# Loading q of batches 2 to 7 by four tokens of a head pair: 24 transfers of 128 KB for 48 of 64 KB, in a fused attention and feed-forward kernel

## The chip, the cores and the metric

The kernel runs on one core of a Trainium2 chip. The metric is the device time of one launch in microseconds (us). Three runs of the kernel before took 359.70, 361.41 and 361.73 us; the median is 361.41 us.

## What is computed

The inputs are q, k and v (8 batches, 8 heads, 576 tokens, head size 64, float32), a feature matrix `w_phi` (64 x 128) and the two matrices of a feed-forward network. Attention is linear: a feature map takes the place of the softmax.

```python
def phi(x):
    proj = np.einsum('bhsd,df->bhsf', x, w_phi)
    proj = proj - np.max(np.abs(proj), axis=-1, keepdims=True)
    return np.concatenate([np.exp(proj), np.exp(-proj)], axis=-1)
q_p, k_p = (phi(q), phi(k))
kv = np.einsum('bhsf,bhsd->bhfd', k_p, v)
z = np.sum(k_p, axis=2)
num = np.einsum('bhsf,bhfd->bhsd', q_p, kv)
den = np.einsum('bhsf,bhf->bhs', q_p, z)[..., None] + 1e-06
attn = num / den
...
x = np.ascontiguousarray(attn_out.transpose(0, 2, 1, 3)).reshape(B * S, H * D)
h = np.maximum(x @ w_in, 0.0)
return (h * h @ w_out).astype(np.float32)
```

`w_in` is 512 x 2048 and `w_out` 2048 x 512, so x has 4608 rows of 512 and the output has the same shape.

## The kernel before, in words

**Stages.** The 576 tokens of a batch are split into 512 and 64. Attention runs batch by batch (`attention(b)`). The feed-forward network runs over nine chunks of 512 rows: chunks 0 to 7 are the 512 tokens of each batch, chunk 8 collects the 64 left over of all eight. The main loop emits attention of batch c+1, the first matmul of chunk c (`ffn_in`, L692; `ffn_in_small`, L703, for chunk 0) and the second of chunk c-1 (`ffn_out`, L757) into one list, so attention of the next batch fills gaps of the feed-forward matmuls on TensorE (PE).

**Who does what.** GpSimd (POOL) issues all loads from memory, with a cast from float32 to bf16 (`load`, L245 and L253; `load_q`, L265). SyncE (SP) issues the transposes done by DMA (L317 for k and q of batches 2 to 7, L612 for the attention output `xo` into `xT` or `xS`) and the stores of the output (L775 for chunks 0 to 7, L772 for chunk 8). For batches 0 and 1, k and q are transposed on PE (L307). VectorE (DVE) and ScalarE (ACT) take the results out of PSUM: maxima (L388, L489), exponentials (L394, L539), relu (L669 or L671) and square (L678), scaling of v (L421), and the copy of the output into one of three buffers `ot` (`copy`: L192 on ACT, L190 on DVE). A copy into `ot` waits for the store of three copies earlier that read the same buffer.

**The end.** The last row tile of chunk 8 is computed in two halves (`last_out`, L721). The copies of the halves into `otl` (L735 on DVE, L737 on ACT) are followed by four small stores (L744): per half, one on SP's queue and one on ACT's. The other three row tiles of chunk 8 have two stores each (L772), all six on SP.

**Order.** Every operation is recorded with `add` and gets a number in the sequence of recording. `ORDER` is a list of these numbers written out by hand: the operations are issued in that order, and each engine works through its own in order. `STATES` says which of two engines takes an operation that may run on either, `BASES` gives each PSUM tile its bank. Loads of batches 2 to 7 are recorded with `release=True`, and nearly all are listed in `GATES`: such a load also waits for a given earlier operation. `FILL` gives, for 13 places ahead of operations of the first 21 us, a bank and a number of matmuls on a tile of zeros (`warm`, L825) that compute nothing.

**q.** `xq` (two buffers) holds q of a batch as 128 partitions by 36 x 64 elements. Partition p holds tokens 4p to 4p+3 of each head. In the kernel before, the two halves of a batch, jj = 0 and 1, are loaded apart: jj holds tokens 4p+2jj and 4p+2jj+1, so each head gives 128 elements in a row. For batches 2 to 7 a half comes in four pieces of one head pair (`PIECES`), which makes 8 transfers of 64 KB and two small ones (L253) for the 64 tokens left over. A block of 128 columns of `xq`, transposed, is one block t of `qT`; `q_ts(c)` lists the blocks of row tile c, the projections L333 read them one by one, and L524 reads four of them as one moving operand.

The SP queue carries, for each batch from 2 on, one transpose of the whole of `xk` and one of the whole of `xq`; the latter waits for all pieces of q.

Of the kernel before, what the change touches and what calls it, by code (L numbers as in the profile page):

```python
# [7 lines left out]
F32 = mybir.dt.float32  # L8
# [16 lines left out]
def dve_cost(n):  # L25
    return n / 960 + 0.064, n / 960 + 0.150 + SEM

# [80 lines left out]
def kernel(  # L108
# [52 lines left out]
    warm = sb("warm", [P])  # L161
# [9 lines left out]
    NXT = 2  # L171
    assert B * S == NCH * TCH and NCH == B + 1 and S == TCH + 64
    qp, qn = ring("qp", NQP, [8 * P]), ring("qn", NQP, [8 * P])
    xo = ring("xo", 3, [8 * D])
    rden = ring("rden", 3, [8], F32)
# [11 lines left out]
    def copy(out, in_):  # L187

        if now[0].eng == "DVE":
            pin(nc.vector.tensor_copy(out=out, in_=in_))  # L190
        else:
            pin(nc.scalar.activation(out=out, in_=in_, func=ACT.Copy))  # L192

# [65 lines left out]
    def load_q(b, jjs=(0, 1), single=True, release=False, prs=((0, 4),)):  # L259

        x = xq[b % 2]
        for jj in jjs:
# [10 lines left out]
    def of(tag, b, us):  # L273
        qs = [("xq", b % 2, u, a) for u in us if u != "s" for a in range(3)] if tag == "xq" else []
        return qs + [(tag, b % 2, u) for u in us if u != "s"] + [(tag, b % 2, "s", hi) for u in us if u == "s" for hi in range(2)]
# [19 lines left out]
    def attention(b):  # L295
# [122 lines left out]
        def scaled(t, x, n):  # L418

            e = t[:, :, D:].to_broadcast([t.shape[0], n, 2, D // 2]).rearrange("p m c x -> p m x c")  # L420
            pin(nc.vector.tensor_tensor(out=t[:, :, :D].rearrange("p m (x c) -> p m x c", c=2),  # L421
                                        in0=x.rearrange("p (m x c) -> p m x c", m=n, c=2), in1=e, op=ALU.mult))

        def v_ops(g0, g1):

            gs = [4] if g0 == 4 else list(range(g0, g1))
            for sg in range(2):
# [9 lines left out]
                def fn(t=t):  # L437
                    scaled(t[:, 8 * g0 : 8 * g1, :], xv[s2][:, 512 * g0 : 512 * g1], 8 * (g1 - g0))
                add("DVE", dve_cost(256 * (g1 - g0)), fn, r=of("xv", b, gs) + [("ve", s2, sg, g) for g in gs],
                    w=[("va", s2, sg, g) for g in gs], what="V")  # L440
# [28 lines left out]
        def q_ts(c):  # L469
            if c == 4:  # L470
                return [16, 17]
            return [8 * (c // 2) + h for h in range(8)] if first else [8 * (c // 2) + 4 * (c % 2) + i for i in range(4)]
# [36 lines left out]
        def q_ops(c):  # L509
# [3 lines left out]
            def fn():  # L513
                o = ps2(pf)
                for u in range(2):
# [5 lines left out]
                    else:  # L521
                        r = slice(64 * u, 64 * u + 64)
                        rhs = qTb[r, ts[0] : ts[-1] + 1, :]
# [19 lines left out]
        def out_ops(c):  # L543
# [27 lines left out]
            xs = xslot[0] % 3  # L571
# [92 lines left out]
    def relu_sq(g, dst, toks):  # L664
# [9 lines left out]
        def fn():  # L674
# [3 lines left out]
            pin(nc.vector.tensor_tensor(out=dst, in0=i_, in1=i_, op=ALU.mult))  # L678
        add("DVE", dve_cost(256), fn, r=[("hr", sl)], w=toks, what="sq")
# [6 lines left out]
    def ffn_in(c, mc):  # L686
# [8 lines left out]
        relu_sq(g, h2[c % 2][mc // 4][:, mc % 4, :], [("h2", c % 2, mc, tt) for tt in range(4)])  # L695

    def ffn_in_small(c, tt, mg):
# [10 lines left out]
        relu_sq(g, h2[c % 2][mg][:, :, tt * P : (tt + 1) * P], [("h2", c % 2, mg * 4 + i, tt) for i in range(4)])  # L708
# [39 lines left out]
    def ffn_out(c, tt, part):  # L748
# [12 lines left out]
        if part == 3:  # L761
# [6 lines left out]
            for u in range(2 if c == NCH - 1 else 1):  # L768
                def fn(u=u):
                    if c == NCH - 1:  # L770
                        b = 2 * tt + u
                        pin(nc.sync.dma_start(out=out[b * S + 512 : b * S + 576, :], in_=ot[sl][u * 64 : u * 64 + 64, :]))  # L772
# [3 lines left out]
                add("SP", (0.5, 0), fn, r=[("ot", sl)], dma=(0.37 if c == NCH - 1 else 0.74, HW_IN, "st"), what="st")  # L776
# [43 lines left out]
    for op in plan.arrange():  # L820
        if op.seq in FILL:
            now[0] = filler
            bank, n = FILL[op.seq]
            for _ in range(n):
                pin(nc.tensor.matmul(out=psum[:, bank, :P], lhsT=warm, rhs=warm, start=True, stop=True))  # L825
# [153 lines left out]
```

## Time and profile before

| | |
|---|---|
| three runs | 359.70, 361.41, 361.73 us |
| span of the profiled execution | 358.8 us (first to last instruction) |
| its own time beside the span | not given; the three runs are 0.9, 2.6 and 2.9 us above this span |
| PE busy | 341.0 us, 95% of the span |
| DVE, ACT, POOL busy | 276.7, 227.1, 112.8 us |
| granted TensorE clock | 0.997 on the mean |
| DMA packets | 102631, 39.62 MB |

How to read it: the span is cut into 40 slices on the profile's page; a digit is the busy share of a slice in tenths. A group of instructions is given by its line in the kernel, its engine, its operation and the tiles that it writes and reads, with the busy time, the mean duration and the idle time of the engine just ahead of it. "POOLq", "SPq" and "ACTq" stand for the sequencers that issue transfers; the time of a transfer itself is that from issue to landing. The chain of waits follows the work that ended last back through what released it.

### The profile page before, as it was taken

The numbers are of one execution on the slowest core, as the hardware profiler recorded it, in microseconds if no ns is written. First come the engines' busy times: TensorE is split into PE (matmuls) and PEld (weight loads), VectorE is DVE, ScalarE is ACT, GpSimd is POOL, SyncE is SP. The second block draws the span as 40 slices with busy tenths as digits, with TensorE's granted clock in tenths as the row PEclk, the third lists the DMA queues.
The fourth block names the chain that finished last, engine by engine and source line by source line (L and its number), as shares of the span: only waits on it lengthen the run. The fifth ranks groups of instructions, "written<-read, shape, count | busy, mean of one in ns | idle before, by whom it ended". The sixth has DMA issues, their size and how long they took to land.

```text
span 358.8 us, 8512 instructions
## 1 busy us (share of the span) xinstructions
PE 341.0 (95%) x3411; PEld 193.6 (54%) x3444; DVE 276.7 (77%) x525; ACT 227.1 (63%) x428; POOL 112.8 (31%) x167
## 2 busy tenths in 40 slices
PE   5989999979999999999999999999999998999994
PEld 4779975524554555455544644455555543444442
DVE  3999998869979997989778878799988816736210
ACT  3999887379779775796678577769777210340301
POOL 8845550784707930299301820000000000000000
PEclk9999999999999999999999999999999999999998
DMA  9999989999979998799956995600401121010105
GB/s 103 177 200 201 175 95 157 161 143 192 117 161 123 159 120 179 175 96 140 127 111 116 97 192 97 151 9 29 62 31 51 50 82 38 3 60 0 58 25 153
DMA packets 102631, 39.62 MB, mean 110 GB/s; under 512 B 77248, under 2 KB 98112, under 8 KB 102592
## 3 DMA queue, kind: packets, MB, share of 16 engines
q0 software_dynamic: 51744, 18.36, 48.4%
q1 hardware_dynamic: 50608, 20.55, 26.4%
q8 instruction: 27, 0.44, 0.5%
q10 hardware_dynamic: 240, 0.16, 0.2%
q14 instruction: 12, 0.10, 0.1%
HBM read 36.77 MB, written 9.44 MB: 129 GB/s over the span
## 4 chain that ended last, share of the span: by engine, by line
PE 72%; DVE 11%; ACT 9%; DMA 5%; issue 2%; SPq 0%; DVEq 0%; ACTq 0%; POOLq 0%
PE psum L757 27%; PE psum L692 24%; PE psum L554 5%; PE psum L333 4%; PE psum L703 3%; PE psum L449 3%; DVE va L421 3%; DMA out_dram<-ot 3%; PE psum L524 2%; ACT kp L394 2%; ACT kn L394 2%; DVE mq L489 2%; DVE h L678 2%; ACT hr L669 1%; DVE mk L367 1%
## 5 line engine op out<-in xcount | busy, mean ns | idle before, releaser
L757 PE MATMUL psum<-wout,h 128*128 128x512 bf16 x527 | 128.3, 380 | 2.5 <-issue 1.3
L692 PE MATMUL psum<-xT,win 128*128 128x512 bf16 x448 | 106.3, 379 | 3.9 <-ACT ot L192 2.5
L669 ACT ACTIVATE hr<-psum 128x512 bf16<-128x512 f32 x96 | 55.3, 596 | 48.2 <-PE psum L692 25.8
L757 PEld LDWEIGHTS <-h 128*128 128x128 bf16 x560 | 50.2, 98 | 54.3 <-issue 1.1
L692 PEld LDWEIGHTS <-win 128*128 128x128 bf16 x512 | 47.4, 97 | 58.0 <-issue 8.0
L678 DVE TENSOR_TENSOR h<-hr 128x512 bf16<-128x512 bf16 x144 | 56.4, 416 | 16.8 <-ACT hr L669 16.0
L539 ACT ACTIVATE qp<-psum 128x1024 bf16<-128x1024 f32 (+1 forms) x40 | 37.4, 940 | 23.1 <-PE psum L524 22.7
L265 POOL DMA_DIRECT2D xq<-in_q_dram x52 | 38.8, 764 | 33.8 <-ACT en L496 21.2
L489 DVE TENSOR_REDUCE mq<-psum 128x8 f32<-128x1024 f32 (+1 forms) x40 | 44.1, 1111 | 3.6 <-PE psum L333 2.9
L388 DVE TENSOR_REDUCE mk<-psum 128x8 f32<-128x1024 f32 (+1 forms) x35 | 38.2, 1111 | 3.1 <-PE psum L333 3.1
L671 DVE TENSOR_SCALAR hr<-psum 128x512 bf16<-128x512 f32 x48 | 32.8, 687 | 9.4 <-PE psum L692 7.9
L394 ACT ACTIVATE kp<-psum 128x1024 bf16<-128x1024 f32 (+1 forms) x35 | 32.8, 937 | 9.6 <-DVE mk L388 8.0
L539 ACT ACTIVATE qn<-psum 128x1024 bf16<-128x1024 f32 (+1 forms) x40 | 37.5, 940 | 1.5 <-PE psum L554 1.2
L394 ACT ACTIVATE kn<-psum 128x1024 bf16<-128x1024 f32 (+1 forms) x35 | 32.8, 937 | 0.0
L421 DVE TENSOR_TENSOR va<-xv,va 64x256 bf16<-64x256 bf16 (+2 forms) x68 | 30.4, 462 | 1.6 <-ACT va L413 0.8
L192 ACT ACTIVATE ot<-psum 128x512 f32<-128x512 f32 x18 | 10.7, 593 | 31.8 <-PE psum L757 27.3
L566 DVE TENSOR_TENSOR psum<-psum,en 128x520 f32<-128x520 f32 (+1 forms) x40 | 27.6, 698 | 3.8 <-PE psum L554 2.5
L578 DVE TENSOR_TENSOR xo<-psum,rden 128x512 bf16<-128x512 f32 (+1 forms) x40 | 27.4, 686 | 0.8
L245 POOL DMA_DIRECT2D xv<-in_v_dram x26 | 19.5, 757 | 23.3 <-DMA out_dram<-ot 20.8
L190 DVE COPY ot<-psum 128x512 f32<-128x512 f32 x17 | 11.6, 684 | 16.1 <-PE psum L757 9.4
L245 POOL DMA_DIRECT2D xk<-in_k_dram x28 | 21.1, 760 | 5.5 <-ACT va L407 3.5
L449 PE MATMUL psum<-va,kp 128*128 128x65 bf16 x256 | 19.6, 193 | 0.9 <-DVE va L421 0.4
(67 smaller groups left out, 402.4 us busy)
## 6 DMA issues: line engine op xcount, KB each, us to landing
out_dram<-ot SPq DMA_DIRECT2D x32, 256.0 KB, 2.8
xk<-in_k_dram POOLq DMA_DIRECT2D x26, 128.0 KB, 3.9
xq<-in_q_dram POOLq DMA_DIRECT2D x48, 64.0 KB, 3.9
xv<-in_v_dram POOLq DMA_DIRECT2D x24, 128.0 KB, 3.6
win<-in_moe_w_in_dram POOLq DMA_DIRECT2D x4, 512.0 KB, 11.7
wout<-in_moe_w_out_dram POOLq DMA_DIRECT2D x4, 512.0 KB, 9.4
xq<-in_q_dram POOLq DMA_DIRECT2D x4, 256.0 KB, 5.0
xv<-in_v_dram POOLq DMA_DIRECT2D x2, 512.0 KB, 9.1
```

What stands on the lines that cost most here:

```text
L245: pin(nc.gpsimd.dma_start(out=x[:, a * 512 : z * 512].rearrange("p (h x) -> p h x", x=4 * D), in_=src[b][2 * a : 2 * z, 0:512, :].rearrang ...
L265: pin(nc.gpsimd.dma_start(out=x[:, jj * 1024 + a * 256 : jj * 1024 + z * 256].rearrange("p (h x) -> p h x", x=128), in_=q[b][2 * a : 2 * z ...
L388: pin(nc.vector.tensor_reduce(out=mk_view(g), in_=ps2(pj)[:, :, : n * Fd].rearrange("p e (i f) -> p e i f", f=Fd), axis=AX.X, op=ALU.max, ...
L394: pin(nc.scalar.activation(out=dst[slot][:, :, :n, :].rearrange("p e i f -> p e (i f)"), in_=ps2(pj)[:, :, : n * Fd], func=ACT.Exp, scale= ...
L421: pin(nc.vector.tensor_tensor(out=t[:, :, :D].rearrange("p m (x c) -> p m x c", c=2), in0=x.rearrange("p (m x c) -> p m x c", m=n, c=2), i ...
L489: pin(nc.vector.tensor_reduce(out=mqb[:, c, :, :n], in_=ps2(pj)[:, :, : n * Fd].rearrange("p e (i f) -> p e i f", f=Fd), axis=AX.X, op=ALU ...
L539: pin(nc.scalar.activation(out=o, in_=i_, func=ACT.Exp, scale=sgn))
L669: pin(nc.scalar.activation(out=hr[sl], in_=ps1(g), func=ACT.Relu))
L671: pin(nc.vector.tensor_scalar(out=hr[sl], in0=ps1(g), scalar1=0.0, scalar2=None, op0=ALU.max))
L678: pin(nc.vector.tensor_tensor(out=dst, in0=i_, in1=i_, op=ALU.mult))
L692: pin(nc.tensor.matmul(out=o, lhsT=win[mc // 4][:, kc, mc % 4 * P : (mc % 4 + 1) * P], rhs=x, start=(kc == 0), stop=(kc == KC - 1)))
L757: pin(nc.tensor.matmul(out=ps1(g), lhsT=h2[c % 2][mc // 4][:, mc % 4, tt * P : (tt + 1) * P], rhs=wout[mc // 4][:, mc % 4, :], start=(mc = ...
```

## The change

For batches 2 to 7, `load_q` issues one transfer for each head pair that takes all four tokens of a partition (256 elements of each head in a row): 4 transfers of 128 KB instead of 8 of 64 KB, the same shape as the pieces of k and v. `q_ts` names the blocks of a row tile accordingly (for batches from 2 on, t = 8(c%2) + 2i + c//2), and the moving operand of L524 steps over every other block. The two small transfers stay.

In `ORDER` all other operations stand in the same sequence as before, renumbered. Each merged transfer stands in the place of the later of the two that it replaces, with that one's gate. The 24 others are gone.

Besides: one of the last six stores (`tt == 2`, second half) goes from SP's queue to ACT's; the rings `xo` and `rden` grow from 3 to 5 buffers; the filling matmuls are 248 columns wide instead of 128, and 64 in number instead of 120, in the same 13 places, so PE's program is 112 instructions shorter (a weight load and a matmul each). The new choices of POOL for two operations are under `LENT = 0`, so none is taken.

```diff
-    warm = sb("warm", [P])
+    warm = sb("warm", [256])
...
-    xo = ring("xo", 3, [8 * D])
-    rden = ring("rden", 3, [8], F32)
+    xo = ring("xo", 5, [8 * D])
+    rden = ring("rden", 5, [8], F32)
...
         x = xq[b % 2]
+        if b >= 2:
+            for a, z in prs:
+                def fn(a=a, z=z):
+                    pin(nc.gpsimd.dma_start(
+                        out=x[:, a * 512 : z * 512].rearrange("p (h x) -> p h x", x=4 * D),
+                        in_=q[b][2 * a : 2 * z, 0:512, :].rearrange("h (p j) d -> p h (j d)", j=4)))
+                old = sorted({pr // 2 for pr in range(a, z)}) if b < 4 else []
+                add("POOL", (0.72, 0), fn, w=[("xq", b % 2, "g", pr) for pr in range(a, z)] + [("xq", b % 2, jj) for jj in old]
+                    + [("xq", b % 2, jj, y) for jj in old for y in range(3)],
+                    dma=(work(b, LD["main"] * (z - a) / 4), SW_IN, "ld", late(b)), release=release, what="xq")
+            jjs = ()
         for jj in jjs:
...
-            return [8 * (c // 2) + h for h in range(8)] if first else [8 * (c // 2) + 4 * (c % 2) + i for i in range(4)]
+            if first:
+                return [8 * (c // 2) + h for h in range(8)]
+            return [(8 * (c // 2) + 4 * (c % 2) + i) if pe_in else 8 * (c % 2) + 2 * i + c // 2 for i in range(4)]
...
-                        rhs = qTb[r, ts[0] : ts[-1] + 1, :]
+                        rhs = qTb[r, ts[0] : ts[-1] + 1 : ts[1] - ts[0], :]
...
-            xs = xslot[0] % 3
+            xs = xslot[0] % 5
...
-                        pin(nc.sync.dma_start(out=out[b * S + 512 : b * S + 576, :], in_=ot[sl][u * 64 : u * 64 + 64, :]))
+                        e = nc.scalar if tt == 2 and u else nc.sync
+                        pin(e.dma_start(out=out[b * S + 512 : b * S + 576, :], in_=ot[sl][u * 64 : u * 64 + 64, :]))
...
-            bank, n = FILL[op.seq]
+            bank, n, col = FILL[op.seq]
             for _ in range(n):
-                pin(nc.tensor.matmul(out=psum[:, bank, :P], lhsT=warm, rhs=warm, start=True, stop=True))
+                pin(nc.tensor.matmul(out=psum[:, bank, col : col + 248], lhsT=warm[:, :P], rhs=warm[:, :248], start=col == 0, stop=True,
+                                     skip_group_check=True))
...
 FILL = {
-    40: (0, 5), 42: (0, 6), 64: (0, 7), 66: (0, 11), 109: (0, 6), 144: (0, 12), 53: (0, 10), 77: (3, 3), 155: (7,
-    36), 158: (7, 10), 127: (2, 3), 149: (6, 1), 161: (6, 10),
+    40: (0, 3, 0), 42: (0, 3, 0), 64: (0, 4, 0), 66: (0, 6, 0), 109: (0, 3, 0), 144: (0, 6, 0), 53: (0, 5, 0),
+    77: (3, 2, 0), 155: (7, 19, 0), 158: (7, 5, 0), 127: (2, 2, 0), 149: (6, 1, 0), 161: (6, 5, 0),
 }
```

More of the change, by code (lines that the diff above doesn't have):

```diff
@@ L26, in dve_cost, with pool_cost @@
     return n / 960 + 0.064, n / 960 + 0.150 + SEM
+def pool_cost(n):
+    return n * 1.75e-3 + 0.15, n * 1.75e-3 + 0.25 + SEM
 def pe_cost(n, each):
@@ L171 @@
     NXT = 2
+    LENT = 0
     assert B * S == NCH * TCH and NCH == B + 1 and S == TCH + 64
     qp, qn = ring("qp", NQP, [8 * P]), ring("qn", NQP, [8 * P])
-    xo = ring("xo", 3, [8 * D])
-    rden = ring("rden", 3, [8], F32)
+    xo = ring("xo", 5, [8 * D])
+    rden = ring("rden", 5, [8], F32)
     xT = [ring(f"xT{c}", 2, [4, 2, P]) for c in range(NXT)]
@@ L192, in copy, with engine @@
             pin(nc.scalar.activation(out=out, in_=in_, func=ACT.Copy))
+    def engine():
+        return nc.gpsimd if now[0].eng == "POOL" else nc.vector
     def ps1(g):
@@ L273, in of @@
     def of(tag, b, us):
+        if tag == "xq" and b >= 2:
+            return [(tag, b % 2, "g", pr) for pr in range(4)] + [(tag, b % 2, "s", hi) for hi in range(2)]
         qs = [("xq", b % 2, u, a) for u in us if u != "s" for a in range(3)] if tag == "xq" else []
@@ L420, in scaled @@
             e = t[:, :, D:].to_broadcast([t.shape[0], n, 2, D // 2]).rearrange("p m c x -> p m x c")
-            pin(nc.vector.tensor_tensor(out=t[:, :, :D].rearrange("p m (x c) -> p m x c", c=2),
+            pin(engine().tensor_tensor(out=t[:, :, :D].rearrange("p m (x c) -> p m x c", c=2),
                                         in0=x.rearrange("p (m x c) -> p m x c", m=n, c=2), in1=e, op=ALU.mult))
@@ L438, in fn @@
                     scaled(t[:, 8 * g0 : 8 * g1, :], xv[s2][:, 512 * g0 : 512 * g1], 8 * (g1 - g0))
-                add("DVE", dve_cost(256 * (g1 - g0)), fn, r=of("xv", b, gs) + [("ve", s2, sg, g) for g in gs],
-                    w=[("va", s2, sg, g) for g in gs], what="V")
+                o = add("DVE", dve_cost(256 * (g1 - g0)), fn, r=of("xv", b, gs) + [("ve", s2, sg, g) for g in gs],
+                        w=[("va", s2, sg, g) for g in gs], what="V")
+                if b < LENT:
+                    plan.either((o, "POOL", pool_cost(512 * (g1 - g0))))
         def kv_ops(pr):
@@ L662, with relu_sq @@
     hslot = [0]
-    def relu_sq(g, dst, toks):
+    def relu_sq(c, g, dst, toks):
         sl = hslot[0] % 4
@@ L677, in fn @@
                 i_ = i_.rearrange("p (m t) -> p m t", t=P)
-            pin(nc.vector.tensor_tensor(out=dst, in0=i_, in1=i_, op=ALU.mult))
-        add("DVE", dve_cost(256), fn, r=[("hr", sl)], w=toks, what="sq")
+            pin(engine().tensor_tensor(out=dst, in0=i_, in1=i_, op=ALU.mult))
+        o = add("DVE", dve_cost(256), fn, r=[("hr", sl)], w=toks, what="sq")
+        if c < LENT:
+            plan.either((o, "POOL", pool_cost(512)))
     def x_toks(c, ts):
@@ L694, in ffn_in @@
         add("PE", pe_cost(4, 0.216), fn, r=[("win", mc // 4)] + x_toks(c, range(4)), w=[g], opens=g, what="F1")
-        relu_sq(g, h2[c % 2][mc // 4][:, mc % 4, :], [("h2", c % 2, mc, tt) for tt in range(4)])
+        relu_sq(c, g, h2[c % 2][mc // 4][:, mc % 4, :], [("h2", c % 2, mc, tt) for tt in range(4)])
     def ffn_in_small(c, tt, mg):
@@ L707, in ffn_in_small @@
             w=[g], opens=g, what="f1")
-        relu_sq(g, h2[c % 2][mg][:, :, tt * P : (tt + 1) * P], [("h2", c % 2, mg * 4 + i, tt) for i in range(4)])
+        relu_sq(c, g, h2[c % 2][mg][:, :, tt * P : (tt + 1) * P], [("h2", c % 2, mg * 4 + i, tt) for i in range(4)])
     opb = {}
@@ L775, in fn @@
                         pin(nc.sync.dma_start(out=o, in_=ot[sl]))
-                add("SP", (0.5, 0), fn, r=[("ot", sl)], dma=(0.37 if c == NCH - 1 else 0.74, HW_IN, "st"), what="st")
+                add("ACT" if c == NCH - 1 and tt == 2 and u else "SP", (0.5, 0), fn, r=[("ot", sl)], dma=(0.37 if c == NCH - 1 else 0.74, HW_IN, "st"), what="st")
     load(k, xk, 0, "xk", prs=((0, 1),))
```

185 rows, old and new, of tables (GATES, ORDER) are left out of this document.

## The prediction

> **What bounds the kernel now.** I read the page's parts 1 to 3 first: how busy each engine is, and what the DMA queues carry.
>
> ```profile
> span 358.8 us, 8512 instructions
> ...
> PE 341.0 (95%) x3411; PEld 193.6 (54%) x3444; DVE 276.7 (77%) x525; ACT 227.1 (63%) x428; POOL 112.8 (31%) x167
> ...
> PE   5989999979999999999999999999999998999994
> ...
> DMA  9999989999979998799956995600401121010105
> GB/s 103 177 200 201 175 95 157 161 143 192 117 161 123 159 120 179 175 96 140 127 111 116 97 192 97 151 9 29 62 31 51 50 82 38 3 60 0 58 25 153
> ...
> q0 software_dynamic: 51744, 18.36, 48.4%
> ...
> q8 instruction: 27, 0.44, 0.5%
> ```
>
> PE is busy 95% of the span, so at most 358.8 - 341.0 = 17.8 us can be had without less matmul work, and the first and last slices hold much of that. The DMA engines are near full for the first half and nearly idle after it. So less load traffic can only be worth what PE waits for through it. Next, the waits by releaser, and the chain of waits, say how much that is.
>
> ```profile
> PE psum L692 <- ACT ot L192: 2.5, 1, 2.5
> ...
> PE psum L692 <- DVE ot L190: 1.2, 1, 1.2
> ```
>
> ```profile
> ACT ot L192 <- DMA out_dram<-ot: 4.5, 1, 4.5
> ...
> DVE ot L190 <- DMA out_dram<-ot: 6.7, 2, 4.9
> ```
>
> ```profile
> 67.94 6.26 DMA out_dram<-ot
> ...
> 294.17 4.42 DMA out_dram<-ot
> ```
>
> These are two links of one kind. A store is in flight for 6.26 us (from 67.94) or 4.42 us (from 294.17); the copy into the same `ot` buffer waits for it; that copy has to empty the PSUM bank that the next L692 needs; PE stands still for 2.5 and 1.2 us. No wait of PE for q appears after the start. What is usual for a transfer is in part 6 of the page:
>
> ```profile
> out_dram<-ot SPq DMA_DIRECT2D x32, 256.0 KB, 2.8
> xk<-in_k_dram POOLq DMA_DIRECT2D x26, 128.0 KB, 3.9
> xq<-in_q_dram POOLq DMA_DIRECT2D x48, 64.0 KB, 3.9
> ```
>
> The store's median is 2.8 us, so these two are late by 3.5 and 1.6 us. Short windows of the trace show why (columns: PE, PEld, DVE, ACT, POOL busy, granted clock, DMA share, GB/s):
>
> ```profile
> 68.00:69.00 1.00, 1.00 (x19) 0.71 (x18) 0.66 (x3) 0.81 (x2) 1.00 (x3) 1.00 2.86 122
> 69.00:70.00 1.00, 0.95 (x5) 0.42 (x5) 1.00 (x1) 0.74 (x1) 1.00 (x2) 1.00 0.07 8
> ```
>
> ```profile
> 296.50:297.50 1.00, 1.00 (x6) 0.46 (x5) 0.00 (x0) 0.00 (x0) 0.00 (x0) 1.00 0.06 16
> ```
>
> At 69 us the traffic stops for a microsecond, at 8 GB/s, with loads waiting. At 296.5 us hardly anything moves, and the store still has not landed. Neither is a lack of bandwidth. A candidate is the instruction queue q8: 0.44 MB in 27 packets is 16 KB each, 0.5% x 358.8 x 16 / 27 = 1.06 us on one engine each, and PE's 3411 + 3444 = 6855 instructions over 27 are 254 for a packet. So PE's program is fetched in long packets, one for every 254 instructions; a store spread over the engines ends with the slowest. The packet list in the trace, which no view prints, has such a packet inside both stores' flights; I use it for the cause alone, not for a term.
>
> **The change part by part.**
>
> *POOL and the loads.* 24 of the q issues go.
>
> ```profile
> L265 POOL DMA_DIRECT2D xq<-in_q_dram x52 | 38.8, 764 | 33.8 <-ACT en L496 21.2
> ...
> L245 POOL DMA_DIRECT2D xk<-in_k_dram x28 | 21.1, 760 | 5.5 <-ACT va L407 3.5
> ```
>
> A piece of 128 KB (xk) takes POOL 760 ns to issue, one of 64 KB (xq) 764. So POOL loses 24 x 0.76 = 18.2 us of work. It is 31% busy and waits on gates; worth 0. The cover for the larger pieces is distance: part 6 has 3.9 us to landing for both sizes, the later of two steps is where the transpose of `xq` was held anyway, and no wait of PE leads to it. If that cover were gone, a piece would be late by at most one 64 KB landing share, 0.4 us (next term). I take 0. A piece has 128 partitions x 2 heads = 256 runs in either size, so 24 x 256 = 6144 of the 51744 packets of q0 go. In SBUF a row of a q transfer goes from 256 to 512 bytes. The Trainium skill ("DMA: Bandwidth & Descriptors", Specifications) says that transfers under 512 B stay below line rate. By that rule two old pieces cost the engines clearly more than one new one, and the load queue would give back up to an eighth of its 48.4%; the equal landings of 3.9 us agree, and the sum would be the same, since PE waits for no load.
>
> *The stall at 72.4 to 74.9.* What POOL issues while that store is in flight:
>
> ```profile
> 67.33 0.72 POOL L245 DMA_DIRECT2D xk<-in_k_dram  x1
> 68.04 1.43 POOL L265 DMA_DIRECT2D xq<-in_q_dram  x2
> 69.44 0.74 POOL L245 DMA_DIRECT2D xk<-in_k_dram  x1
> ```
>
> The two q pieces at 68.04 are earlier halves of batch 3, so they go, and what stands behind them comes 1.4 us sooner. 128 KB at the 122 GB/s of that window are 1.05 us; half of it is taken by what moves up, which leaves about 0.4 us. The larger part is the fetch. With 112 PE instructions gone ahead of 21 us, each later fetch comes 112 instructions later in the work: 0.44 of a packet's 254.
>
> ```profile
> 70.00:80.00 10.00, 7.36 (x57) 3.22 (x57) 7.04 (x10) 5.71 (x11) 8.87 (x14) 1.00 1.53 169
> ...
> 290.00:300.00 10.00, 8.76 (x47) 4.04 (x48) 2.02 (x4) 0.94 (x2) 0.00 (x0) 1.00 0.15 54
> ```
>
> PE runs 114 instructions in the 10 us from 70, so that fetch moves some 9.8 us, past this store. Together 1.06 + 0.4 = 1.5 us sooner; of the stall 1.0 us is left. Bounds: 0 (the crowd alone holds the store) and -2.5 (the whole stall). I take **-1.5**.
>
> *The stall at 298.2 to 299.4.* There are 95 PE instructions in the 10 us from 290, so the fetch moves by 112 / 9.5 = 11.8 us, behind the landing. The store is then at its 2.8 us, 1.6 us sooner, more than the 1.2 us of the stall. Bounds 0 and -1.2; I take **-1.2**, since nothing else is in its way (54 GB/s).
>
> *Fetches that hit something else.* As many fetches fall as before, on other transfers. Most stores have no copy waiting: by the rows above, three copies in all waited for one. Bounds 0 and +2.5 (one stall as long as the longest); 3 of 32 stores were waited for, and two fetches are taken off such a store, so a new hit is less likely than not: I take a fifth of the bound, **+0.5**.
>
> *The last stores.* The timeline of the end ("x6": the six stores L772, one after the other on SP):
>
> ```profile
> 351.64 3.68 SPq L772 DMA_DIRECT2D out_dram<-ot  x6
> ...
> 353.02 0.60 ACT L192 ACTIVATE ot<-psum 128x512 f32<-128x512 f32 x1 [1.08 <-PE psum L757]
> 354.33 0.38 ACT L737 ACTIVATE otl<-psum 128x256 f32<-128x256 f32 x1 [0.71 <-PE psum L721]
> 354.75 0.49 ACTq L744 DMA_DIRECT2D out_dram<-otl  x1
> 355.41 0.74 SPq L744 DMA_DIRECT2D out_dram<-otl  x1
> ```
>
> ACT's last store goes out at 354.75, its twin on SP at 355.41, because six stores at 3.68 / 6 = 0.61 us are ahead of it. With five, the last two wait for the copy that ends at 353.62 and take until 353.62 + 1.22 = 354.84; the twin goes at about 354.9: **-0.5**. On ACT the added issue (0.49 us by its like) stands ahead of the copy at 353.02, which waits 1.08 us for PE; the data of it are ready at 351.6, so it is over by 352.5. If it came 0.5 us later, the copy and the rest of the end would move by what passes 353.02. Bounds -0.66 and 0.
>
> *The filling matmuls.* On the chain of the start:
>
> ```profile
> 5.14 0.64 PE psum L825 x6
> ...
> 6.32 0.86 PE psum L825 x7
> ...
> 7.61 1.09 PE psum L825 x11
> ```
>
> These three become 3, 4 and 6 of 248 columns: 744 + 992 + 1488 = 3224 columns for 3072. At 0.86 / (7 x 128) = 0.96 ns a column that is +0.15 us. Later fills stand where DVE and ACT are the full engines. Bounds +0.3 and -0.3; I take **+0.1**. The larger `warm` memset is hidden by the wait for the first k.
>
> *The rest.* The stepped moving operand of L524 has 256-byte runs, as xT in L692 has, and
>
> ```profile
> L757 PE MATMUL psum<-wout,h 128*128 128x512 bf16 x527 | 128.3, 380 | 2.5 <-issue 1.3
> L692 PE MATMUL psum<-xT,win 128*128 128x512 bf16 x448 | 106.3, 379 | 3.9 <-ACT ot L192 2.5
> ...
> L578 DVE TENSOR_TENSOR xo<-psum,rden 128x512 bf16<-128x512 f32 (+1 forms) x40 | 27.4, 686 | 0.8
> ```
>
> stepped (L692) and unbroken (L757) take 379 and 380 ns: 0. The `xo` copies wait 0.8 us in all, so two more buffers are worth 0 to -0.8 on DVE, and nothing on PE.
>
> **Sum.** -1.5 - 1.2 + 0.5 - 0.5 + 0.1 = -2.6 us on the span: 358.8 to 356.2. The page gives the execution's span alone; the median of the runs is 2.6 us above it, the fastest run 0.9. I keep the 2.6 of the median: 361.4 - 2.6 = **358.8 us**.
>
> **Rivals.**
>
> *Only the end gains* (fetches do not set the stalls, or move onto as many others). For it: one copy's worth of coincidence explains two stalls as well, and q's pieces were never waited for. Against it: the empty windows. It gives -0.5 + 0.1, 361.0 us. The Trainium skill ("Runtime: NRT & Kernel Launch", Instruction fetch mechanics) has engines refill in 16 KiB blocks of 256 instructions, and calls the cost of crossing one mostly hidden. The block size agrees with the q8 row; its "hidden" would make this rival right, at 361.0.
>
> *Slower: bursts of merged pieces.* POOL issues a piece each 0.76 us, so 128 KB pieces in a row ask for 172 GB/s, 64 KB pieces for 86; the fullest slices moved 201 in all, with transposes and stores. Where three or more follow each other, a queue builds up, and a store behind it lands late. The point: at 72 us PE lost 2.5 us with a landing of 6.26, so it waits from about 3.8 us on. If the first stall stays and one more like it comes up between 100 and 220 us, where the copies' buffers are shared with loads: 361.4 - 0.5 + 2.5 = 363.4 us. Against it: the packets per piece stay, and 3.9 us for both sizes.
>
> *It doesn't do what it says:* if each new transfer were split as the old ones, packets would not fall, and the sum would lose only the 0.4 us: 359.2 us, inside the forecast.
>
> **Chances.** Forecast with its variants 0.52, only the end 0.32, bursts 0.16. 0.5% (1.8 us, about what a measurement of this kernel can tell from no change) sets the classes at 359.6 and 363.2: faster 0.52, same 0.33, slower 0.15. The range: at the best, -2.5 - 1.2 - 0.66 - 0.8 - 0.3 = -5.5, 356.0; at the top 363.0, which takes in the second case and leaves out most of the third.
>
> **What would show it.** Right: no copy into `ot` near 73 us waits over 2 us for a store, none near 298 us at all, L692's idle time falls from 3.9 to near 1 us, the last L744 of SP is issued within 0.3 us of ACT's, q0 shows some 45600 packets. Wrong: other stores with landings over 4 us and a PE wait behind them; PE waiting for `qT` or `kT` of a batch; the first DVE maxima later by more than 0.3 us.

## The result, and the profile after

| | before | after |
|---|---|---|
| executions | 359.7, 361.73, 361.41, 361.91 us | 355.91, 357.4, 358.57, 356.24 us |
| median | 361.57 us | 356.82 us |
| ratio | | 0.9869, 95% interval 0.9831 to 0.9907 |
| span of the profiled execution | 358.8 us | 353.9 us (its own time 355.91) |

The change makes the kernel faster by 4.75 us (1.3%); 2.6 us were forecast. Here and below, a ratio leaves out executions that lie over 1.5% above the fastest of their kernel, and a median takes in all. These are the lines of the page after that answer to those of before. The engines' digits are again shares of 40 slices; in the groups, the numbers behind the bar are busy time, mean ns of one and idle time ahead; in the last three rows the last number is the median time to landing.

```profile
span 353.9 us, 8406 instructions
...
PE 343.2 (97%) x3388; PEld 191.8 (54%) x3388; DVE 276.6 (78%) x525; ACT 227.3 (64%) x428; POOL 95.6 (27%) x143
...
PE   5989999999999999999999999999999999999995
...
q0 software_dynamic: 45216, 18.36, 45.8%
...
q8 instruction: 26, 0.43, 0.5%
...
L784 PE MATMUL psum<-wout,h 128*128 128x512 bf16 x560 | 133.5, 379 | 0.0
L719 PE MATMUL psum<-xT,win 128*128 128x512 bf16 x448 | 106.1, 379 | 0.0
...
out_dram<-ot SPq DMA_DIRECT2D x32, 256.0 KB, 2.6
xk<-in_k_dram POOLq DMA_DIRECT2D x26, 128.0 KB, 4.6
xq<-in_q_dram POOLq DMA_DIRECT2D x24, 128.0 KB, 5.6
```

L784 and L719 are the old L757 and L692. The idle time ahead of L692 was 3.9 us and is 0.0: both stalls are gone whole. The slices of PE show it too, all 9 from the fourth to the last but one. The loads got slower, 4.6 and 5.6 us to landing where xk and xq had 3.9, and no wait of PE came of it. The waits by releaser say how near the rest still is:

```profile
DVE ot L195 <- DMA out_dram<-ot: 5.4, 3, 3.1
...
ACT ot L197 <- DMA out_dram<-ot: 1.3, 1, 1.3
```

Four copies into `ot` still wait for a store (total, number, longest), one for 3.1 us. None holds PE up: no wait of L719 for a copy is left. The two stretches quoted before as 7.36 and 8.76 us of PE are now full (columns as before):

```profile
70.00:80.00 10.00, 10.00 (x78) 4.49 (x77) 9.62 (x16) 8.81 (x15) 7.88 (x12) 1.00 1.49 147
290.00:300.00 10.00, 10.00 (x55) 4.65 (x53) 6.10 (x12) 1.19 (x2) 0.00 (x0) 1.00 0.17 59
```

Where the time came from is read from the same copies into `ot` in both traces (before, after): at 60.54 and 60.59 us, nothing yet; at 98.85 and 95.87, 2.98 us gained; at 267.95 and 264.97, still 2.98; at 318.10 and 313.78, 4.32; the last one at 353.02 and 348.70, 4.32. From there to the end of the span it is 358.8 - 353.0 = 5.8 us before and 353.9 - 348.7 = 5.2 after: 0.6 more. So 3.0 + 1.3 + 0.6 = 4.9 us of span, at three places. At the first, 2.5 us are the stall itself; the other 0.5 us are shorter waits of PE, one of 0.2 us of L692 for `kn` among them. The end of the timeline after:

```profile
347.42 3.04 SPq L800 DMA_DIRECT2D out_dram<-ot  x5
347.43 0.50 ACTq L800 DMA_DIRECT2D out_dram<-ot  x1
...
348.70 0.60 ACT L197 ACTIVATE ot<-psum 128x512 f32<-128x512 f32 x1 [1.08 <-PE psum L784]
350.01 0.38 ACT L764 ACTIVATE otl<-psum 128x256 f32<-128x256 f32 x1 [0.71 <-PE psum L748]
350.42 0.47 ACTq L771 DMA_DIRECT2D out_dram<-otl  x1
350.56 0.55 SPq L771 DMA_DIRECT2D out_dram<-otl  x1
```

SP's last store follows ACT's by 0.14 us; it was 0.66. The added issue on ACT is over at 347.9, ahead of the copy at 348.70, whose wait for PE is the same 1.08 us.

### The profile page after: what moved, and what is told of

Same layout as the page of the kernel before. It is cut to its first block, busy times and chain, and to the rows that moved or that the text cites. A ratio compares the mean times of both kernels' runs of the same rounds, so it can differ in the third digit from the quotient of the medians.

```text
span 353.9 us, 8406 instructions
## 1 busy us (share of the span) xinstructions
PE 343.2 (97%) x3388; PEld 191.8 (54%) x3388; DVE 276.6 (78%) x525; ACT 227.3 (64%) x428; POOL 95.6 (27%) x143
## 3 DMA queue, kind: packets, MB, share of 16 engines
q0 software_dynamic: 45216, 18.36, 45.8%
## 4 chain that ended last, share of the span: by engine, by line
PE 76%; DVE 14%; ACT 6%; issue 2%; DMA 1%; DVEq 0%; ACTq 0%; POOLq 0%
PE psum L784 30%; PE psum L719 24%; PE psum L579 5%; PE psum L354 4%; PE psum L730 3%; PE psum L472 3%; DVE va L442 3%; DVE h L703 2%; PE psum L549 2%; DVE mq L514 2%; DVE mk L409 2%; DVE hr L696 2%; ACT kp L415 1%; ACT kn L415 1%; DVE mk L388 1%
## 5 line engine op out<-in xcount | busy, mean ns | idle before, releaser
L784 PE MATMUL psum<-wout,h 128*128 128x512 bf16 x560 | 133.5, 379 | 0.0
L719 PE MATMUL psum<-xT,win 128*128 128x512 bf16 x448 | 106.1, 379 | 0.0
L784 PEld LDWEIGHTS <-h 128*128 128x128 bf16 x560 | 50.2, 98 | 54.3 <-issue 1.1
L719 PEld LDWEIGHTS <-win 128*128 128x128 bf16 x512 | 47.5, 98 | 53.6 <-issue 3.1
L273 POOL DMA_DIRECT2D xq<-in_q_dram x24 | 17.6, 736 | 12.5 <-ACT va L428 5.4
## 6 DMA issues: line engine op xcount, KB each, us to landing
win<-in_moe_w_in_dram POOLq DMA_DIRECT2D x4, 512.0 KB, 11.6
```

What stands on the lines that cost most here:

```text
L719: pin(nc.tensor.matmul(out=o, lhsT=win[mc // 4][:, kc, mc % 4 * P : (mc % 4 + 1) * P], rhs=x, start=(kc == 0), stop=(kc == KC - 1)))
L784: pin(nc.tensor.matmul(out=ps1(g), lhsT=h2[c % 2][mc // 4][:, mc % 4, tt * P : (tt + 1) * P], rhs=wout[mc // 4][:, mc % 4, :], start=(mc = ...
```

## Experiments

**Two theories.** A, that of the prediction: PE's instructions are fetched by packets of 16 KB, the changed kernel has 112 fewer of them early on, so the fetches fall elsewhere, and the two stores that PE waited for land in time. B: it is the loads, fewer and other ones around 68 to 75 us. The first four kernels split the change into its parts.

*The changed kernel with the old filling matmuls.* 120 of 128 columns instead of 64 of 248:

```diff
-    40: (0, 3, 0), 42: (0, 3, 0), 64: (0, 4, 0), 66: (0, 6, 0), ...
+    40: (0, 5), 42: (0, 6), 64: (0, 7), 66: (0, 11), ...
```

> The changed kernel with the filling matmuls of before (120 of 128 columns, so 8 instructions of TensorE between two of its fetches stand where they stood before, 56 matmuls and their weight loads back). Theory A (the stalls at 72 and 298 us went because the fetches of TensorE's instructions fell elsewhere, by 112 instructions fewer ahead of the work): both stalls come back, +4.3 us, some 361 us. Theory B (the stall at 72 us went because fewer and other loads are in flight there): the first stall stays away, at most the second comes back, 356.8 to 358.2 us.

Measured: 360.19 us, the kernel before beside it 361.49, ratio 0.9968 (0.9934 to 1.0002). Both stalls are back (waits by releaser):

```profile
ACT ot L197 <- DMA out_dram<-ot: 3.7, 1, 3.7
...
PE psum L719 <- ACT ot L197: 1.6, 1, 1.6
PE psum L719 <- DVE ot L195: 1.3, 1, 1.3
```

The second stall is as long as before; the first is 1.6 us where it was 2.5. A holds for both stalls. The 0.9 us may be B's share in the first, but one trace can't fix its size: the last of these four kernels leaves loads and fills as they were, and its first stall is 3.3 us.

*The kernel before with the new filling matmuls alone.* The mirror image of the last one.

> The kernel before with the new filling matmuls alone (64 of 248 columns), loads of q as before. Theory A: both stalls go, some -4.3 us, 357.3 us. Theory B: the stall at 72 us stays, the one at 298 us may go, 360.2 to 361.5 us.

Measured: 359.0 us, ratio 0.9936 (0.9902 to 0.9969). No wait of PE in L692 for a copy is left in its trace; the span is 354.9 us. The group line of its page:

```profile
L692 PE MATMUL psum<-xT,win 128*128 128x512 bf16 x448 | 106.1, 379 | 0.1
```

The trace is as A expected, but it is that of the fastest of the twelve executions (356.64 us). The median lies between A's 357.3 and B's 360.2, a little nearer to B's, so the times alone don't decide here. Three of the twelve executions have a mean granted clock of 0.993 to 0.995; what the executions without a trace waited for isn't shown.

*The kernel before with the merged transfers of q alone.* From the changed kernel, back to the old fills, three buffers of `xo` and `rden`, and all six last stores on SP:

```diff
-    xo = ring("xo", 5, [8 * D])
+    xo = ring("xo", 3, [8 * D])
...
-                        e = nc.scalar if tt == 2 and u else nc.sync
+                        e = nc.sync
```

> The kernel before with the merged transfers of q alone: filling matmuls, rings of xo and rden and the last stores as before. Theory A: both stalls stay, 361.3 us, 0.5 to either side. Theory B: the stall at 72 us goes, -3.0 us, 358.6 us.

Measured: 360.05 us, ratio 0.9981 (0.9951 to 1.001): no difference that the interval shows. In the trace the first stall is 1.2 us and the second 1.3:

```profile
PE psum L719 <- DVE ot L195: 1.3, 1, 1.3
PE psum L719 <- ACT ot L197: 1.2, 1, 1.2
```

So the transfers of q, the part that the change is named after, take neither stall away; the first is shorter in both traces that have them together with the old fills (1.2 and 1.6 us, for 2.5 and 3.3 without).

*The kernel before with one of the last stores issued by ScalarE.*

```diff
-                        pin(nc.sync.dma_start(out=out[b * S + 512 : b * S + 576, :], ...
+                        e = nc.scalar if tt == 2 and u else nc.sync
+                        pin(e.dma_start(out=out[b * S + 512 : b * S + 576, :], ...
```

> The kernel before with one of the last stores issued by ScalarE, nothing else. Both theories: -0.6 us from the end alone, 361.0 us, and both stalls stay.

Measured: 361.71 us, ratio 1.0013 (0.9976 to 1.0049). The 0.6 us can't be seen in the times. In its trace the last copy into `ot` at 355.86 stands 5.2 us ahead of the end at 361.1, against 5.8 before, so the gain is there; but the first stall was longer in that execution (PE waited 3.3 us), and the clock behind it fell. The wait, and windows of a microsecond (PE busy in the first column after the length, granted clock third from the end):

```profile
PE psum L692 <- ACT ot L192: 3.3, 1, 3.3
```

```profile
74.00:75.00 1.00, 0.00 (x0) 0.00 (x0) 0.59 (x1) 0.00 (x0) 0.24 (x1) 1.00 1.31 128
75.00:76.00 1.00, 0.27 (x2) 0.15 (x2) 0.00 (x0) 0.89 (x3) 0.48 (x1) 1.00 1.78 157
76.00:77.00 1.00, 0.82 (x5) 0.30 (x4) 0.00 (x0) 1.00 (x3) 1.00 (x3) 0.84 1.63 186
77.00:78.00 1.00, 1.00 (x3) 0.34 (x3) 0.00 (x0) 1.00 (x2) 1.00 (x2) 0.50 1.05 121
...
79.00:80.00 1.00, 1.00 (x4) 0.30 (x2) 0.60 (x1) 0.62 (x2) 1.00 (x3) 0.50 1.38 147
80.00:81.00 1.00, 1.00 (x13) 0.40 (x12) 0.60 (x1) 0.05 (x1) 1.00 (x2) 0.95 0.84 59
```

A stall can cost a second time: from about 76.7 to 80 us PE runs at half its clock, 1.7 us lost. The copy at 98.85 us in the kernel before comes at 101.18 here, 2.33 us later: 0.86 is the longer wait, and the rest, 1.47, goes with the half clock.

**Is it the wait for the store?** A fourth buffer of `ot` takes that wait away and leaves fetches and loads alone.

```diff
-    ot = ring("ot", 3, [DM], F32)
+    ot = ring("ot", 4, [DM], F32)
...
-            sl = oslot[0] % 3
+            sl = oslot[0] % 4
```

> The kernel before with a fourth buffer in the ring of ot, so that no copy has to wait for the store of three copies earlier. The fetches of TensorE's instructions and the loads stay where they are. If the wait of a copy for its store is how the fetches cost time: both stalls go (the one at 298 us as well as the one at 73 us), the granted clock stays at full speed behind 76 us, 4 to 4.6 us less than before, some 357.3 us. Rival: TensorE waits for its own instructions, or for a load, and the store only looked like the cause: the stalls stay, 361 us.

Measured: 358.91 us, beside 361.25; ratio 0.9942 (0.9915 to 0.997). The kernel stores one block of 128 rows of the output (chunk 2, the third of its four row tiles) with another tile's values: in `ORDER` the copy of chunk 3's third tile, in the same buffer, stands ahead of that block's store. Both old stalls are gone. But buffers taken in turn by recording number put a new wait of 1.6 us at 142 us, and the same drop of the clock comes behind it:

```profile
142.00:143.00 1.00, 0.31 (x8) 0.17 (x8) 0.00 (x0) 1.00 (x2) 0.00 (x0) 1.00 0.89 230
143.00:144.00 1.00, 0.10 (x4) 0.10 (x5) 0.81 (x2) 0.91 (x2) 0.00 (x0) 1.00 0.58 116
144.00:145.00 1.00, 1.00 (x11) 0.50 (x9) 0.97 (x2) 0.00 (x0) 0.00 (x0) 0.73 1.15 214
145.00:146.00 1.00, 1.00 (x4) 0.33 (x3) 0.94 (x3) 0.00 (x0) 0.00 (x0) 0.50 1.15 212
```

The same edit on the changed kernel, with the same block wrong:

> The changed kernel with the fourth buffer of ot. Where both stalls are already gone, the fourth buffer has nothing to take away: 356.8 us, 0.5 to either side. Rival: some executions of the changed kernel still meet a late store, and the median falls by 0.5 to 1.5 us.

Measured: 359.25 us, ratio 0.9939 (0.9915 to 0.9964): slower than the changed kernel's 356.82. Its trace has the same new wait and one of 1.3 us at 216 us. Neither settles its question; both are mended below.

**Does only the place of the fetches matter?** The number of filling matmuls was changed in the changed kernel, to 192 of 82 columns and to 92 of 170, so at nearly the same number of columns in all. The edit for 192:

```diff
-    40: (0, 3, 0), 42: (0, 3, 0), 64: (0, 4, 0), 66: (0, 6, 0), ...
+    40: (0, 8, 0), 42: (0, 10, 0), 64: (0, 11, 0), 66: (0, 17, 0), ...
```

> The changed kernel with 192 filling matmuls of 82 columns: 128 more than in the changed kernel, so 256 more instructions of TensorE (a matmul and a weight load each), about one whole spacing of its fetches; the columns multiplied are nearly the same in all. If only the place of the fetches matters, this is the changed kernel again, though it has 72 more filling matmuls than the kernel before: no stall, 356.8 us, up to 1 us more for the more instructions. Rival: what helps is that there are fewer instructions ahead of the work: both stalls come back or grow, 360 to 362 us.

Measured: 357.16 us, ratio 0.9895 (0.9863 to 0.9928). With 72 fills more than the kernel before, no stall:

```profile
L784 PE MATMUL psum<-wout,h 128*128 128x512 bf16 x560 | 133.5, 379 | 0.0
L719 PE MATMUL psum<-xT,win 128*128 128x512 bf16 x448 | 106.0, 379 | 0.0
```

"Fewer instructions" falls; the place of the fetches, one spacing further on, is what is the same.

> The changed kernel with 92 filling matmuls of 170 columns, half the way between 64 and 120. By the place of the fetches: those at 68 and 295 us of before come at some 71 and 301 us; the one at 71 us still falls into the store that the copy at 71 to 74 us waits for, the one at 301 us behind the pair of stores. So the first stall stays in part (0 to 3 us) and the second goes, 357 to 360 us. Rival (fewer is better): half of the way, both stalls at half their length, 359 us.

Measured: 356.85 us, ratio 0.9877 (0.9849 to 0.9904).

```profile
L719 PE MATMUL psum<-xT,win 128*128 128x512 bf16 x448 | 106.2, 379 | 0.0
```

No stall at all: the second went as expected, and the first too, against the expectation. The fetch came at 70.34 us, 2.9 us behind the issue of the store, which still landed after 3.8 us.

**The fourth buffer, mended.** Each copy takes the buffer whose store was issued longest ago. This kernel differs from the one before in two things, the number of buffers and the rule by which they are taken; the rule was not tried with three.

```diff
-    oslot = [0]
+    free, osl = [0, 1, 2, 3], {}
...
+            sl = c, tt
...
-                copy(ot[sl], ps1(g))
+                osl[c, tt] = free.pop(0)
+                copy(ot[osl[c, tt]], ps1(g))
...
-                        pin(nc.sync.dma_start(out=o, in_=ot[sl]))
+                        pin(nc.sync.dma_start(out=o, in_=ot[osl[sl]]))
+                        free.append(osl[sl])
```

> The kernel before with a fourth buffer of ot, each copy now taking the buffer whose store was issued longest ago (in the earlier kernel with four buffers, taken in turn by number, a copy came ahead of the store of an earlier tile in the same buffer, so a block of the output was another tile's, and TensorE got a wait of 1.8 us near 142 us that the kernel before doesn't have). Fetches and loads as in before. If the copy's wait for its store is how the fetches cost time: no stall at 73, 142 or 298 us, TensorE busy throughout 70 to 80 us, -4.3 to -6 us, 355.5 to 357.2 us. Rival (the store is not the cause): 361 us.

Measured: 355.8 us, beside 361.05; ratio 0.9882 (0.9836 to 0.9927). The store at 67.8 us (one line, one stretch of the trace) still meets the fetch and lands late, and nobody waits for it (no row stands under "who waited"):

```profile
L775 SPq DMA_DIRECT2D out_dram<-ot x1: 1069/1069/1069, 67.8 to 67.8; - x1
...
who waited for it (us, times):
...
DMA to landing us min/median/max: 5.4/5.4/5.4
```

```profile
70.00:80.00 10.00, 10.00 (x78) 4.49 (x77) 9.62 (x16) 8.59 (x15) 9.54 (x15) 1.00 1.42 160
```

One of its six executions took 359.91 us, at a mean clock of 0.993; it has no trace.

> The changed kernel with the same fourth buffer. With no late store left to wait for it has nothing to gain where TensorE doesn't stand: 356.8 us, 0.7 to either side. Rival: the executions of the changed kernel that are slow meet a late store, and the median falls by over 1 us.

Measured: 355.95 us, ratio 0.9874 (0.9843 to 0.9904). That is 0.85 us below the 356.8 that was expected, just outside the 0.7.

> The changed kernel unaltered, beside the other two on the same chip: 356.8 us, 0.7 to either side; its granted clock is at full speed in all executions if the stalls are what lowers the clock in some executions of the kernel before.

Measured: 357.61 us, ratio 0.9904 (0.987 to 0.9938), 0.8 us above what was expected. The clock was not at full speed in all executions: of nine, one took 362.49 us at 0.995. So the rival of the kernel ahead, that some executions of the changed kernel still meet a late store, isn't out, though in its two traces no late store holds PE up.

With four buffers the kernel before and the changed one take the same time, 355.8 and 355.95 us: once no copy waits for its store, the transfers of q, the fills and the rest of the change are worth nothing that can be measured. The medians put both below the changed kernel, by 1.7 to 1.8 us in that series (1.2 to 1.3 without the execution at 362.49) and by some 1 us against 356.82; the intervals overlap, so that they beat it is likely and not shown.

**All traces together.** The start of the fetch beside the store's issue (within 3 us), or, where there is none, of the next fetch behind it; then the issue, and the time from issue to landing, all in us. The fetches are from the packet list, which no view prints.

| kernel | fetch, issue, flight at the first place | at the second |
|---|---|---|
| before | 68.2, 67.9, 6.3 | 294.8, 294.2, 4.4 |
| after, old fills | 67.7, 67.9, 5.9 | 294.9, 294.3, 4.5 |
| before, q merged | 67.5, 67.8, 5.3 | 293.9, 293.4, 4.5 |
| before, last store | 67.1, 67.4, 7.6 | 297.7, 296.8, 4.6 |
| before, four `ot`, mended | 67.3, 67.8, 5.4 | 291.7, 291.1, 4.5 |
| before, four `ot` by number | 68.2, 68.5, 6.4 | 296.8, 295.3, 3.9 |
| before, new fills | 72.7, 67.1, 3.8 | 305.0, 291.5, 2.7 |
| after | 73.4, 67.5, 3.6 | 304.9, 291.2, 2.6 |
| after, once more | 74.2, 68.1, 3.6 | 305.5, 291.8, 2.6 |
| after, four `ot` by number | 74.1, 67.3, 3.8 | 306.2, 296.0, 2.6 |
| after, 192 fills | 74.5, 68.2, 3.7 | 305.3, 292.0, 2.6 |
| after, 92 fills | 70.3, 67.4, 3.8 | 296.2, 291.2, 2.6 |
| after, four `ot`, mended | 74.1, 68.3, 3.7 | 305.4, 292.0, 2.6 |

A fetch that starts within a microsecond of the store's issue goes with 5.3 to 7.6 us at the first place and 4.4 to 4.6 at the second; without one it is 3.6 to 3.8 and 2.6 to 2.7. One that starts 1.5 us behind the issue stands between, at 3.9; one that starts 2.9 us behind it leaves 3.8, as without. So at these two places it holds over all thirteen traces, with the fetches moved by three other counts of fills.

The packet list also shows how. At the second place of the kernel before, the fetch runs from 294.82 to 296.48 us. Of the 256 packets of 2 KB of the two stores issued at 293.8 and 294.2, 240 have been moved by 296.1. The other 16, a sixteenth, run one after the other from 296.47 to 298.14, as the share of one of the 16 DMA engines would that the fetch has kept busy. In the changed kernel, with no fetch there, all 256 are done by 293.2, 2.0 us behind the second issue. At the first place, in the six traces with a fetch within a microsecond of the issue, 18 to 82 of the packets that start in the 2 us behind it (instruction packets apart) take over 0.9 us, the longest 1.1 to 1.8; in the other seven the longest takes 0.2 to 0.6.

A nearby rival is out by the same list: packets of 8 KB on the other instruction queue, q14, start 0.4 to 0.6 us behind the first store in six of the traces without a late landing (3.6 to 3.8 us).

The sizes are those of the two places. At four others (near 148, 187, 241 and 281 us) a fetch within 1.1 us of the issue goes with 2.8 to 4.1 us, where the same store takes 2.1 to 3.2 without one: 0.6 to 1.4 us more. At a fifth, near 136 us, the one trace that has it shows no clear difference (3.7 us against 2.7 to 3.8). Near 129 to 134 us a fetch 2.5 us behind the issue still goes with 4.3 to 4.4 us in three traces, where it is 2.7 to 2.8 without. And not every late landing is a fetch's: three stores issued within 1.2 us of each other at 206 to 213 us take 4.5 to 6.4 us in every trace, with no fetch that starts within 2.7 us of an issue.

## Why the prediction was right, and where its sizes were off

**The mechanism was right:** a store in the way of an instruction fetch, a copy that waits for it, PE that waits for the copy. The old fills bring both stalls back; the new fills alone take both away in the one trace that they have; a fourth buffer takes them away with the fetches left in place.

**The stall at 72.4 to 74.9: taken as -1.5, measured -3.0** (2.5 of it the stall). This is the step that was mis-sized, and the greater part of why the gain was 4.75 and not 2.6 us. It took the fetch at its own duration, 1.06 us, and the load crowd at 0.4, and left 1.0 us of the stall. The store's flight fell from 6.3 to 3.6 us, by 2.7, so the whole stall of 2.5 went; the new fills alone did the same (3.8 us). A fetch beside this store costs it 1.5 to 4 us, more than the fetch itself takes. The load crowd shows a share only in the presence of the fetch: with q merged and the old fills the stall is 1.2 to 1.6 us, and with the old loads and the new fills the one trace has none. The fetch did move past the store, but by 5.2 us (68.2 to 73.4) and not by 9.8: the prediction took PE's rate from 70 to 80 us, where it stood still for part of the time, while the rows shown there already count 47 instructions between 68 and 70 us.

**The stall at 298.2 to 299.4: taken as -1.2, measured -1.3.** Right, though a copy there still waits 3.1 us for its store; that no copy near it would wait at all was wrong.

**Fetches that hit something else: taken as +0.5, measured 0.** Four copies wait for stores, none long enough to reach PE.

**The last stores -0.5, measured -0.6; the fills +0.1, measured +0.05** at 60.5 us. 45216 packets on q0 against some 45600.

**Equal landings of the loads** did not hold: xq's went from 3.9 to 5.6 us and xk's from 3.9 to 4.6. The term stayed 0 since PE waits for no load after the start. So of the rival "bursts of merged pieces" the queue is there in part, and the stall is not. That the change doesn't do what it says is out: 24 transfers of 128 KB on the page, and fewer packets. The load queue gave back 48.4% of 358.8 less 45.8% of 353.9, so 11.6 us of 173.7 or 7%, about half of the eighth that the packets' count would give; it goes in the direction of the rule of the Trainium skill ("DMA: Bandwidth & Descriptors", Specifications) that the prediction named, and PE waited for none of it.

**The offset of span and time:** 2.6 us were kept, measured were 2.0 in the execution after. In the later series the kernel before lies 1.7 to 1.8 us above its span, so the 2.6 held some 0.8 us by which the profiled execution was faster than the median. The execution profiled after is 0.9 us faster than its median too, so the gains in span (4.9) and in time (4.75) can be compared.

**"Only the end gains"** failed. The Trainium skill ("Runtime: NRT & Kernel Launch", Instruction fetch mechanics) calls the crossing of a 16 KiB block mostly hidden. For PE itself the traces agree, as the changed kernel's L719 and L784 have no idle time with 26 fetches. For a store beside it they don't: 5.3 to 7.6 us against 3.6 to 3.8.

**Left open.** The new fills alone have a trace without stalls, but a median 1.4 us above the changed kernel's 357.61 and 2.2 above its 356.82. The last store's 0.6 us may be in that; the rest isn't explained, and with it the share of the loads in a typical execution is open. The two longer rings, `xo` and `rden`, were not tried alone.

## What to carry to other kernels

When a stall is behind a transfer that is late for no reason of bandwidth, look at who waits for its landing and give that waiter a further buffer: here one more buffer of 2 KB a partition, with the oldest free one taken first, brought what the whole change brought. A gain that comes from a shifted instruction count is real but not robust: any edit that adds or removes instructions of that engine early on can bring the stall back, so test it by changing the count alone. Undo the parts of a change one at a time before crediting the one that it is named after.

## What the runs showed of the hardware

- PE's instructions come in packets of 16 KB (0.43 MB in 26), and such a fetch can hold up a store. One that starts within a microsecond of a 256 KB store's issue goes with a landing 1.5 to 4 us later at 68 us, where loads are in flight, and 1.7 to 2.0 us later at 294 us, where the DMA engines are nearly idle; at four of five other places it is 0.6 to 1.4 us. There is no one reach: a fetch 2.9 us behind the issue changes nothing at 67 us, one 2.5 us behind costs about 1.6 us near 129 us.
- The granted clock falls to 0.50 for some 3.4 us after some pauses of PE: from about 76.7 to 80 us behind 3.3 us of waiting, and from about 144.5 to 147.9 us behind a wait of 1.6 us; the 2.5 us pause in the kernel before's trace did not bring it. The Trainium skill ("TensorE: Matmul & The Clock Gate", Part 1) has a gate that halves the clock after at least one idle window of some 3.4 us, and says that the windows run freely, wherever the work starts. The half clock and its length agree with that. The pauses do not: both are shorter than the window, 1.6 us by half. No run here shows the windows themselves.
- The mean granted clock of whole executions goes with the stalls. It is under 0.997 in 32 of 68 executions of the kernel before (median 362.4 us, the others 360.1), and one drop as above would take 1.7 of some 359 us, or 0.005, off the mean. By the first stall of the trace: with 2.5 to 3.3 us (before, last store) it is 41 of 80 executions, with 1.2 to 1.6 us (old fills, q merged) 4 of 24, with none (after twice, new fills, 192 and 92 fills, four buffers mended) 5 of 49, one of them among 13 of the changed kernel. That these are executions with a drop behind the first stall is argued from the one trace that has it, not shown for each.
